# A new order of issue for a bucketed attention and Mish feed-forward kernel on one core

## The chip, the cores and the metric

The kernel runs on one core of a Trainium2 chip. The metric is the device time of one execution in microseconds (us); the median of three runs before the change is 817.67 us (816.54 to 818.07). Engines are named as in the profile: PE (TensorE, matmuls), PEld (its weight loads), DVE (VectorE), ACT (ScalarE), POOL (GpSimd) and SP (SyncE, which here only issues DMAs).

## The reference

Four batches of eight heads, 768 positions, 64 channels. Queries and keys are hashed to six bits each; a query sees only the keys of its own bucket.

```python
q_bits = einsum('bhsd,dk->bhsk', q, proj) > 0          # k_bits in the same way
mask   = q_bucket[:, :, :, None] == k_bucket[:, :, None, :]
scores = where(mask, q @ k.T / sqrt(64), -1e9)
attn   = exp(scores - max(scores)); attn /= sum(attn) + 1e-9
x      = (attn @ v), heads laid side by side           # 3072 x 512
h      = x @ w_in                                      # 512 -> 2048
g      = h * tanh(log1p(exp(h)))                       # Mish
out    = g @ w_out                                     # 2048 -> 512, fp32
```

## The kernel before

The host program does not write instructions straight down. It records 2,636 small operations in a plan (`Plan.op`, L44): each has a name, one or more forms with the engine that each runs on, and the operations that must come before it. Then `Plan.ordered` (L76) walks one long table, `ORDER` (L93): a number is an operation, a letter behind it the form to take (none or a is the first form, b to d the next). The schedule is manual, so each engine's instructions stand in the program in the order in which the table names them, and each engine works through its own row strictly in that order; semaphores between engines come from the recorded dependences. SP issues every DMA, loads and stores and transposes alike, so the transfers queue in table order too. Whenever the next ACT operation needs the other function table (exp or Mish), `ordered` puts a table load (L1315) ahead of it, so the table's order also sets how many loads there are.

The work is cut so that many small pieces interleave. There are 12 units of attention (three for each batch) with eight score blocks each; S0 to S95 count them. One score block goes through this chain:

- S: eight matmuls on PE into a wide PSUM tile `ps_s` (L937; the first blocks in fp32, L948), two heads side by side, 128 queries by 768 keys each. Hash agreement is folded into the product.
- max: one reduction on DVE over 128 x 1536 (L978).
- mb: the scale and the bias for exp, made of the maximum and a threshold. It has four forms: on DVE on both heads at once (L961 and L968), on DVE head by head (two variants, L961 with L968 or L965), or on POOL (L972 and L973).
- exp: two activations on ACT out of `ps_s` (L991), with the row sums.
- rv, hi and lo: the reciprocal (L1021) and the split of the weights into two fp16 parts; hi on POOL (L390), ACT (L392) or DVE (L393), lo on DVE (L408) or POOL (L414, L415).
- transposes by DMA (L472), and for each pair of blocks V: 72 matmuls (L1088).

The feed-forward follows some units behind: X is split (L1096, L1099), H is 24 matmuls (L1130 to L1132), mish runs on ACT (L1147, L1151), its result is split again, and O, an output block, is 6 matmuls for each half (L1179 to L1181), evicted by ACT or DVE (L1197, L1203) and stored (L1207). Between these lie preparations for the next batch: squares for norms on ACT (L480), hash products (L739), splits of inputs and weights.

The start is a chain of its own: loads of K and Q, a unit matrix on POOL (masks.py lines), warm-up matmuls of a tile of ones on PE (L364), transposes on PE against the unit matrix (L450, copied out by L453), a hash projection (L461) by a small matrix `pw` that DVE makes (L530), and the first score blocks in fp32.

Of the kernel before, what the change touches and what calls it, by code (L numbers as in the profile page):

```python
# [93 lines left out]
137 7 9 8 50 20 0 5 11 19 12 22 1 2 3 4 76 80 29 81b 13 37 6 77b 14 15 10 25 33 26 30b 38 17 27 28 18 34 39 52  # L94
60 61 35 62 41 56 54 63 57 55 21 42 48 51 53 24 23 31 78 36 32 64 65 16 86 91 138 92 79 87 147 40 88 82 117 83
43 118 44 119b 93 89 66 109 110 111 153 90 94 120 67 112 154b 132 107d 46 108 133 113 95 115 68 114 116 124
125b 155 121 126 101 84 45 134 136 135 156 127b 178 96 128 140b 148 141 47 58 149 85 122d 123 97 99 142 139b
98b 143 129 168d 179 180d 100 174 176 69 175 177 170 130 157 171b 131 172 173b 204 205b 169 70 145b 182 189
144b 102 158 159 181 161b 190b 71 193 291 194 195 185 191 150 186 192 220 221 103 222d 183b 187 206 160b 196
188 197 104 223 212 152 146 49 151 162 59 105 106 213b 207 216 218 217b 219b 214 215b 184 353 224 243 163 239  # L100
164 244 245b 241 248 240 242 233c 270 368 307 210d 208 235 254 236 255 249 209b 237 246 238 247 225 256 271
250 257 234 272d 262 263 268 266 292 198 273 226 267b 211 227 293 165 294 269 251 283 284 349 350 264 303 265
285 295 166 304b 354 305 296 258 199 200 309d 286b 310 311c 260c 261 306 274 281 313 253 252 232 228 282 312b
322 201 317 364 287 365 288 289 290 366 318 319 355b 323 324 308 320 321 367 330b 331 315 338 339 72 231 203
202 167 229 397 369b 314 329 316 325 297 298b 275 276b 340 333 341 230 332b 334 342 73 370d 299 336 425c 277
# [12 lines left out]
692 628 693d 572 624b 643b 782 672 644 645c 646 695 694 669 610b 658 723c 724 629 630b 684b 687 696 734 735
670b 673 783 697 675 725b 727 736d 738 686 726 631 698 737 688 690 689 732 786 731 749 674 667 699c 701 729
740d 741 791 742c 744 676 728 787 788 700 750 751 702 730 745 799 703 704 706 743b 677b 671 678 746 739 733  # L120
803 781 752 753 773b 800 784c 774 776 775 785 790 679b 804 705b 707 708 710 709 711 794 748 824 712 801c 779
777b 795 796c 802b 789 713 792 714c 716 780 747 778 825 839 680 798 797 816c 817 818b 715b 819 826 827 828 829
820 822 830 807 808 842 611 717 754 755 821 847 823 810 831b 832 833b 809 811 756 757 805 843 844 845 835 846
840 718 859 841 836 834c 719 721b 720b 758 759 860 722 760 837 838 769 861 871 872 863 873b 874 812 862b 864
875 876d 806 813 762 866 793 877 887 891 888 761 889b 892 865 879b 895 763 867 896 897d 898 848 878c 882 890b
880 868 884 904 764 765 885b 893c 899 883 881 849 850c 900 770 923 766b 852b 913b 914 771 767 922 908 924 768
925 905 901 915 916 926 917 927 928c 853 772 909 918 894 919 1026 920 929 930c 906 939 932b 910 902b 911 912
940 814b 869 968 854 921 972 941d 943 942 954 851c 903 931c 934 907 855 857 945 946 856 955 956c 947b 949b 969
973 1027 957 958 959c 937 936 982 970c 1028 933 935 960 961 948b 951b 858 971 963 976 815 944 977 978 979c 950
# [1216 lines left out]
```

## Time and profile before

| | |
|---|---|
| median of the runs | 817.67 us (816.54 to 818.07) |
| profiled execution | 817.2 us, its span 815.4 us, granted clock 1.00 |
| PE busy | 798.2 us (98%) |
| DVE busy | 602.9 us (74%) |
| ACT busy | 624.9 us (77%), of it 150.1 us in 117 table loads |
| POOL busy | 426.9 us (52%) |
| DMA traffic | 134.29 MB, mean 165 GB/s |

All times are from one profiled execution. A row of a timeline gives start, duration, engine, line, operation, result <- operands, shapes, and in brackets the idle time of the engine ahead of it with what ended it. In a list of groups the numbers behind the bar are busy time in us and mean ns of one instruction, then idle time ahead. In a list of waits stand the waiting engine and line, what it waited for, total us, times and the longest. A busy PE is not necessarily PE at its peak, as matmuls overlap: eight score matmuls last 1.46 us alone, but the next block starts 1.30 us after the first.

### The profile page before, as it was taken

To read this page: it belongs to the slowest core of one execution; us is meant where nothing else is said; L and a number is where in the kernel's file an instruction comes from. 1 tells how busy PE (TensorE), PEld (TensorE's weight loads), DVE (VectorE), ACT (ScalarE), POOL (GpSimd) and SP (SyncE) were. 2 spreads that over 40 slices of the span, in tenths; PEclk is the share of its full clock that TensorE was granted. 3 is DMA by queue.
4 is the path that set the end of the run, shared out by engine and by line. 5 is a ranking of instruction groups with operands and counts; after the bars stand their busy time and mean duration, and the time that the engine had idled before them with its cause. 6 is when DMAs were issued, how large, how long until landed. Compare 5 with 4: busy or idle time off the path is not lost.

```text
span 815.4 us, 17000 instructions
## 1 busy us (share of the span) xinstructions
PE 798.2 (98%) x6546; PEld 549.6 (67%) x6546; DVE 602.9 (74%) x1103; ACT 624.9 (77%) x976; POOL 426.9 (52%) x434
## 2 busy tenths in 40 slices
PE   8899999999999999999999999999999999999998
PEld 5556666666676776676666676667676676776674
DVE  5888999988898778887887767768877675566211
ACT  4889998888696769889679698989779785677211
POOL 3564446554356773733585564344646758845120
PEclk9999999999999999999999999999999999999999
DMA  7958998989999969989989959999989577466200
GB/s 253 219 174 221 240 246 196 191 156 206 217 160 182 203 116 181 170 158 216 185 172 155 195 117 151 197 213 192 167 140 169 107 139 145 81 124 133 50 27 27
DMA packets 395489, 134.29 MB, mean 165 GB/s; under 512 B 365456, under 2 KB 386448, under 8 KB 395408
## 3 DMA queue, kind: packets, MB, share of 16 engines
q1 hardware_dynamic: 395408, 133.21, 81.2%
q8 instruction: 51, 0.84, 0.4%
q14 instruction: 30, 0.25, 0.1%
HBM read 35.65 MB, written 6.29 MB: 51 GB/s over the span
## 4 chain that ended last, share of the span: by engine, by line
PE 47%; ACT 1%; DVE 1%; DMA 1%; issue 0%; POOL 0%; SPq 0%; ACTq 0%; DVEq 0%
PE ps_s L937 7%; PE ps_o L1179 6%; PE ps_o L1181 6%; PE ps_o L1180 6%; PE ps_acc L1130 5%; PE ps_t L1088 5%; PE ps_acc L1132 5%; PE ps_acc L1131 5%; ACT pb L991 1%; DVE svb L978 1%; DMA out_dram<-ffb 1%; PE ps_t L739 0%; ACT L1315 0%; DVE hl L408 0%; ACT tok L480 0%
## 5 line engine op out<-in xcount | busy, mean ns | idle before, releaser
L991 ACT ACTIVATE pb<-ps_s,svb 128x768 f32<-128x768 f32 x184 | 180.9, 987 | 87.4 <-DVE svb L968 36.7
L978 DVE TENSOR_REDUCE svb<-ps_s 128x2 f32<-128x1536 f32 x92 | 161.3, 1753 | 40.2 <-PE ps_s L937 33.7
L1130 PE MATMUL ps_acc<-X,wo 128*128 128x256 f16 x616 | 167.9, 273 | 0.3 <-ACT ffb L1151 0.3
L1132 PE MATMUL ps_acc<-X,wo 128*128 128x256 f16 x616 | 167.9, 273 | 0.0
L1131 PE MATMUL ps_acc<-X,wo 128*128 128x256 f16 x616 | 167.9, 273 | 0.0
L1315 ACT ACT_TABLE_LOAD x117 | 150.1, 1283 | 2.0
L408 DVE SCALAR_TENSOR_TENSOR hl<-pb,svb,hl 128x768 f16<-128x768 f32 x131 | 140.3, 1078 | 13.8 <-POOL hl L390 9.8
L1181 PE MATMUL ps_o<-wi,ffb 128*128 128x512 f16 x352 | 133.4, 379 | 0.0
L1180 PE MATMUL ps_o<-wi,ffb 128*128 128x512 f16 x352 | 133.4, 379 | 0.0
L1179 PE MATMUL ps_o<-wi,ffb 128*128 128x512 f16 x352 | 133.4, 379 | 0.0
L937 PE MATMUL ps_s<-KT,QT 128*128 128x512 f16 (+1 forms) x656 | 120.1, 326 | 2.1 <-ACT pb L991 1.8
L390 POOL TENSOR_SCALAR hl<-pb,svb 128x768 f16<-128x768 f32 x68 | 71.0, 1046 | 75.9 <-DVE svb L1021 28.8
L937 PEld LDWEIGHTS <-QT 128*128 128x128 f16 x672 | 64.2, 98 | 40.5 <-issue 8.3
L1088 PE MATMUL ps_t<-PT,VT 128*64 128x256 f16 x1584 | 90.7, 273 | 0.0
L1088 PEld LDWEIGHTS <-VT 128*64 128x64 f16 x1584 | 84.8, 110 | 8.1 <-issue 7.6
L1151 ACT ACTIVATE ffb<-ps_acc,smalls 128x512 f32<-128x512 f32 x88 | 58.5, 684 | 33.5 <-PE ps_acc L1132 32.0
L415 POOL TENSOR_TENSOR hl<-pb,hl 128x768 f16<-128x768 f32 x45 | 75.0, 1667 | 3.8
L414 POOL TENSOR_SCALAR pb<-pb,svb 128x768 f32<-128x768 f32 x45 | 44.4, 987 | 48.0 <-ACT hl L392 21.4
L1131 PEld LDWEIGHTS <-wo 128*128 128x128 f16 x616 | 60.2, 98 | 13.3 <-issue 1.5
L1130 PEld LDWEIGHTS <-wo 128*128 128x128 f16 x616 | 60.2, 98 | 12.6 <-issue 0.5
L1132 PEld LDWEIGHTS <-wo 128*128 128x128 f16 x616 | 60.2, 98 | 7.0
L1181 PEld LDWEIGHTS <-ffb 128*128 128x128 f16 x352 | 34.4, 98 | 41.6
(240 smaller groups left out, 1300.5 us busy)
## 6 DMA issues: line engine op xcount, KB each, us to landing
out_dram<-ffb SPq DMA_DIRECT2D x22, 256.0 KB, 2.7
stg<-in_v_dram SPq DMA_DIRECT2D x13, 384.0 KB, 4.0
stg<-in_k_dram SPq DMA_DIRECT2D x12, 384.0 KB, 4.0
wo<-in_q_dram SPq DMA_DIRECT2D x9, 512.0 KB, 4.9
stg<-in_moe_w_in_dram SPq DMA_DIRECT2D x8, 512.0 KB, 4.6
stg<-in_moe_w_out_dram SPq DMA_DIRECT2D x6, 512.0 KB, 4.6
PT<-hl SPq DMA_TRANSPOSE x176, 4.1
wo<-in_moe_w_out_dram SPq DMA_DIRECT2D x5, 512.0 KB, 4.7
```

The lines of the kernel that those rows point to most:

```text
L408: return [("DVE", 215 + 1.035 * n, port(lambda: nc.vector.scalar_tensor_tensor(out=dst, in0=src, scalar=sc, in1=hi, op0=ALU.mult, op1=ALU. ...
L937: nc.tensor.matmul(ps[:, hh * S + c0 * P:hh * S + c1 * P], QTb[:, u % 2, sl, qi], KTb[:, j, sl, hh * NCH + c0:hh * NCH + c1].rearrange("p ...
L978: op("max", [("DVE", 1755, lambda: nc.vector.tensor_reduce(out=sv[:, 0], in_=ps.rearrange("p (h e) -> p h e", e=S), axis=AX.X, op=ALU.max, ...
L991: EXP[n, hh] = op("exp", [("ACT", 1075, lambda hh=hh, t=t: nc.scalar.activation(pb[:, t], HOMES[n][0][:, hh * S:(hh + 1) * S], AF.Exp, bia ...
L1088: nc.tensor.matmul(pv[hh * D:(hh + 1) * D, y * 256:(y + 1) * 256], vt[:, w, hh * NCH + c], pt[:, hh, a * NCH + c].rearrange("p s t -> p (s ...
L1130: nc.tensor.matmul(o, wh, X[:, 0, c], start=(c == 0), stop=False)
L1131: nc.tensor.matmul(o, wh, X[:, 1, c], start=False, stop=False)
L1132: nc.tensor.matmul(o, wl, X[:, 0, c], start=False, stop=(c == NCC - 1))
L1179: nc.tensor.matmul(PS[f"o{s}"], gh, wh, start=first, stop=False)
L1180: nc.tensor.matmul(PS[f"o{s}"], gh, wl, start=False, stop=False)
L1181: nc.tensor.matmul(PS[f"o{s}"], gl, wh, start=False, stop=last)
L1315: for fn in plan.ordered("exp", lambda x: nc.scalar.preload_act_table_set(sets[x])):
```

## The change

Only the table `ORDER` differs. Both tables name all 2,636 operations once. 2,501 of them stand at another place, by nine places on the mean and 251 at most, and 483 have another letter, that is another form or engine for the same operation. No operation, buffer or transfer is new. Because forms and places differ, so do some counts: the scale and bias (mb) run on POOL 33 times where they ran there 22 times, and ACT has 109 table loads where it had 117.

```diff
 ORDER = """
-137 7 9 8 50 20 0 5 11 19 12 22 1 2 3 4 76 80 29 81b 13 37 6 77b 14 15 10 25 33 26 30b 38 17 27 28 18 34 39 52
...
+8 7 9 50 19 20 12 22 11 18 10 0 1 2 80 3 29 4 33 25 13 37 54 26 34 30b 52 48 60 57 56 17 81b 5 6 31 32 27 38
...
```

First place, DVE at the start. `ones` feeds the warm-ups, `ffb` is the unit matrix here, KT and QT are transposed inputs, pw the hash matrix. Before:

```order
L358 MEMSET ones 128x128
L358 MEMSET floors 128x1
L453 COPY KT<-ps_t 128x384
L358 MEMSET floors 128x4
L453 COPY KT<-ps_l 128x384
L501 TENSOR_SCALAR smalls<-ps_t 128x1
L485 TENSOR_SCALAR smalls<-smalls 128x1
L375 TENSOR_REDUCE smalls<-ffb 128x1
L377 TENSOR_SCALAR smalls<-smalls 128x1
L453 COPY KT<-ps_s 128x384
```

In the change:

```order
L358 MEMSET smalls 128x1
L375 TENSOR_REDUCE smalls<-ffb 128x1
L377 TENSOR_SCALAR smalls<-smalls 128x1
L358 MEMSET ones 128x128
L453 COPY KT<-ps_s 128x384
L530 TENSOR_SCALAR pw<-pj_79 64x6 x4
L453 COPY KT<-ps_t 128x384
```

The reduction over the unit matrix now stands ahead of the memset of ones, and pw behind the first of the three copies; before, pw stood behind all three and four more instructions.

Second place, POOL at the start (`tok_65` is a tile that is cleared once; L972 and L973 are mb). Before:

```order
L795 MEMSET wo 128x12x64
masks.py:197 MEMSET ffb 128x128
masks.py:199 ISA
masks.py:199 AFFINE_SELECT ffb<-ffb 128x128
L358 MEMSET pw 128x128
L358 MEMSET tok_65 128x2048
L390 TENSOR_SCALAR tok_64<-wi,smalls 128x8x64
```

In the change:

```order
L358 MEMSET tok_65 128x2048
masks.py:197 MEMSET ffb 128x128
masks.py:199 ISA
masks.py:199 AFFINE_SELECT ffb<-ffb 128x128
L358 MEMSET pw 128x128
L414 TENSOR_SCALAR PT<-PT,smalls 128x768
L415 TENSOR_TENSOR wo<-PT,wo 128x12x64
L972 TENSOR_SCALAR svb<-svb,smalls 128x2
L973 TENSOR_TENSOR svb<-svb 128x2
L972 TENSOR_SCALAR svb<-svb,smalls 128x2
L973 TENSOR_TENSOR svb<-svb 128x2
L795 MEMSET wo 128x12x64
```

The large clear has moved ahead of the unit matrix, a split of a key tile has come to POOL, and the first two scale-and-bias pairs as well.

Third place, ACT about the score block S24, whose exps are the L991 row behind the last table load of each piece. Before:

```order
L1315 ACT_TABLE_LOAD
L1151 ACTIVATE ffb<-ps_acc_782,smalls 128x512
L392 ACTIVATE hl<-pb,svb 128x768 x2
L392 ACTIVATE VT<-stg,smalls 128x768
L1151 ACTIVATE ffb<-ps_acc_783,smalls 128x512
L480 ACTIVATE tok_64,smalls<-stg 128x768 x2
L1315 ACT_TABLE_LOAD
L991 ACTIVATE pb,svb<-ps_s,svb 128x768 x2
```

In the change:

```order
L480 ACTIVATE tok_64,smalls<-stg 128x768
L1012 ACTIVATE svb<-svb 128x2
L392 ACTIVATE hl<-pb,svb 128x768
L1315 ACT_TABLE_LOAD
L1151 ACTIVATE ffb<-ps_acc_779,smalls 128x512
L480 ACTIVATE tok_64,smalls<-stg 128x768
L1151 ACTIVATE ffb<-ps_acc_780,smalls 128x512
L1315 ACT_TABLE_LOAD
L991 ACTIVATE pb,svb<-ps_s,svb 128x768 x2
```

The two squares (L480) stood together straight ahead of the exp table load; now the first is ahead of the Mish table load and the second between two mish.

More of the change, by code (lines that the diff above doesn't have):

```diff
@@ new lines @@
+350 264 303 265 285 261 304b 199 258 294d 295 296 286b 200 309b 310 311b 355 312b 305 253 167 252 232 203 274
+281b 308 282 306 313 228 322 201 231 323 317 364 287 365 288 289 290 366 318 319 315 324 259 320 321 367 325
+357 338 229 397 399 369b 314 202 330c 297 331 275 339 230 276b 298b 333 332b 334 340 341 342 370d 316 329 328
+335 299 425c 336 277 426 398 300 278 400 302 280 301 337 378 423 424 351 371 373c 379 380 381 372b 374 382
+389c 427 411 376 428 452 390 352 406 407 375 279 391 383 384b 412 451 73 392c 393 74 408d 409 343 410 415d
@@ new lines @@
+628 639 708 572 782 672 643b 641 669 644 645c 646 696 693d 694 695 657b 723d 687 658 624c 667 724 725b 629b
+610 673 734 735 686 727 736d 630b 679b 697 675 737 738 677b 783 726c 689 786 731 690 749 678b 688 728 631 698
+674 699c 701 729 740b 741 670b 742 743 787 750 744 676 751d 733 799 702 730 703 745 700c 790 732 803 739 753
+752 784c 704 706 705b 707 709 671 746b 710 773c 774 776b 775 777 785 791 779 800 801 711 794 748 747 778 780
+712 781 824 795 825 713 796 714c 716 680 788 804 789 797 798 816d 817 819 792 818 826 827 828c 829 820 822 802
@@ new lines @@
+830 807 839 808 810 805 715b 806b 831d 832 809 811 812 754 755 611 717 756 757 821 823 642 847 842 843 844 845
+833b 835 846 860d 840 859 758 841 759 834c 718 836 837 719 861 769 871 872 884 770 891 887 838 863 760b 721b
+720b 862b 722 864 873d 874 875 876d 865 885b 813 771 762 866 772 877 895 888 892 896 763 867 900 764 904 868
+761b 878 848 889 879b 893 897d 882 883 898 880 881 899 849 765 766 894 767 850c 890 913b 914 852 923 924 925
+901 915b 917 916c 902c 926 927 814 922 908 768 853 919 920 918 1026 939 928 929 793 815 905 909 911 910 906b
@@ new lines @@
+1017 870 1223 1195 988b 1070 1018 1038 1196 1082 1073 1042b 1052d 1053 1043 1054 1055c 1044 1056 989 1057c
+1059 1045b 1058c 1046 1060 1077 1061b 1078 1079c 1083 1074 1081 1080 1063 1020 1086 1064 1035b 1067 1068 1071c
+1072 1075c 1197 1036 1084c 1095c 1096 1098b 1097 1099b 1062 1105 1047 1090 1106 1107c 1108 1109 1101 1110 1085
+1111 1121 1122 1087 1091 1048 1076b 1198 1112c 1123 1124 1114 1125 1150 1151 1088b 1127d 1037 1065 1100 1113c
+1158 1116 1102 1154 1136 1104 1103 1128 1092 1200 1155 1137 1115 1117 1129b 1130c 1138 1131 1139 1132 1140
@@ new lines @@
+1141c 1133 1093 1142 1143b 1145 1134 1146 1119 1168 1159 1160 1161 1163 1162 1177c 1144b 1147 1152c 1153 1126
+1118 1164 1178 1094 1169 1179 1187 1188 1189 1190 1181 1191 1207c 1208 1148 1049 1201 1120 1172 1180b 1183b
+1156 1089b 1165 1166 1157b 1209c 1211 1218 1199 1219 1220b 1173 1175 1224 1182 1210b 1213b 1184 1252 1212 1174
+1225 1176 1226c 1222 1221 1236d 1237 1238 1149 1135 1240b 1228 1186 1185 1216 1202 1247 1282 1215 1278 1248
+1249c 1250 1251 1203 1239c 1205 1214 1253 1229 1241 1286 1204b 1242 1267d 1170 1171 1268 1279 1167b 1283 1287
@@ new lines @@
+1269b 1280 1281 1271 1270 1243 1206 1291 1230 1235 1295 1288d 1273 1231 1289 1290 1318 1405 1308b 1227c 1309
+1310c 1233 1312 1254 1255 1284b 1217 1256 1275 1319 1320d 1272 1274 1257 1258 1232b 1260 1311 1321 1322 1338b
+1299 1296 1300 1276b 1304b 1292 1293b 1285 1301 1339 1234 1306 1349 1244 1340b 1259b 1350 1314 1351d 1294b
+1313 1261 1342 1341c 1315 1245 1302 1303 1353 1352 1355c 1401 1397 1356 1305 1344b 1402 1398 1297b 1246 1343
+1324 1345 1323 1364 1365 1366d 1316 1367 1357c 1358c 1359 1368 1325 1326 1418 1262 1317 1409 1361 1388 1263
@@ new lines @@
+1389 1390c 1264b 1265b 1392b 1410 1411b 1406 1399c 1414 1347 1327 1346 1412 1413 1431c 1462 1360 1391c 1394
+1362 1393 1395 1266 1441 1348 1354 1403c 1298 1328 1329c 1432 1331 1442 1443c 1433b 1435 1444 1369 1363 1422
+1332 1307 1400b 1445 1446c 1434c 1437 1370 1415 1423 1447 1425 1419 1416c 1448b 1330b 1450b 1424 1426 1371
+1372 1396 1457 1333 1334 1458 1440 1439 1459b 1373 1502 1374 1335b 1404 1336b 1460 1461 1375 1475 1476 1377
+1438 1436 1449 1451 1486 1337 1378 1506 1477 1503 1504b 1515 1379 1454 1452 1407 1479 1487 1488 1490 1489 1277
@@ new lines @@
+1453 1505 1417 1507 1376b 1478b 1420c 1491 1380 1481 1382b 1381b 1480 1510 1463 1492 1493c 1511 1512d 1464
+1495 1421 1513 1514 1455 1465b 1494c 1497 1528 1529 1408 1384 1467 1383 1482 1496 1519 1456 1498 1468 1641
+1538 1385 1474 1483 1520 1587 1499 1530b 1539 1386 1540 1532 1531c 1508b 1469 1470 1466c 1516 1541 1542 1543c
+1427b 1534b 1471b 1509 1544 1554 1545 1523 1555 1591 1387 1547 1533 1583 1521b 1642 1556d 1558 1524 1557 1569
+1522b 1517 1518b 1546b 1549b 1682 1560c 1472 1526 1500 1537 1484 1588 1525 1561 1570 1571 1548 1563 1584 1536
@@ new lines @@
+1535 1473 1550 1552 1551 1572 1562b 1564 1573 1574c 1597 1559 1428 1527 1566 1429b 1575 1430 1565 1501 1576
+1592 1553 1601 1582 1577 1585c 1578b 1643 1644 1593 1594 1567 1596 1595 1610c 1580 1586 1646 1681 1611 1579
+1568 1620 1618 1621 1645 1598 1613 1599b 1622b 1616 1581 1485 1605 1619 1683 1589 1600 1590 1623 1647 1612b
+1614b 1624 1625 1626 1627c 1629b 1615 1636 1628b 1631b 1633 1634 1635 1606 1637 1607 1638c 1868 1630 1617 1632
+1608 1602 1609 1648 1603 1653 1640 1639 1654c 1655 1656 1657c 1665 1666 1667 1668 1658 1669 1688 1684 1660
@@ new lines @@
+1792c 1783 1747 1767 1759b 1813 1762 1749 1761 1763 1734 1735 1802 1741 1771c 1815 1768 1793 1795 1814 1803
+1804 1805 1787 1764 1794b 1796 1806 1798 1822d 1772b 1823 1824c 1826b 1867 1816 1664 1797 1799 1827 1780 1790
+1839 1788 1833 1801 1750 1834 1835d 1840 1841 1789 1791 1843 1831 1817 1800 1784 1837 1836 1851c 1862 1852
+1853c 1818 1820 1819b 1855b 1854c 1863 1864b 1825 1828 1866 1865 1785b 1781b 1882c 1844 1821 1857 1842c 1782
+1856 1829 1893 1897 1901 1830 1845 1869 1870 1902 1883 1885c 1903 1786b 1884 1858 1680 1832 1904 1886 1905
@@ new lines @@
+2004 1946 2005c 2007 2024 2025 2026c 2028 2027 2046c 1984 1947 1977 2033 1969 1963 2008 1948 2056 1949 2015
+2018 2006b 1945b 1913b 2011 1986 1987 1951 2057 2009b 2010 1950b 2019b 1988 1978 2055 1989 2047 2048c 2034
+2030 2031b 2049 1990c 2058 2050 2060 2059 2061c 1992 2052 1999 2032 2062 2063c 2037 2072 1861 1952 1991b 2038
+2040 2039 2041 1993 2051 2053 2070 1994 2121 2089 2073 2022 2074 2078 2065b 2075 2076 2064b 2122 2090d 2035
+2036b 1995 2067 2079 2080 2091 2092 2066 2101 1892 2068 2102 2103 2093 2104 2094 2105 2106c 2117 2000 2114
@@ new lines @@
+2054 2082 2107 2096 2023 2125 2069 2134 2071 2126 2001 2206 2002 1996b 2127d 2108 2128 2110 2129 2123 2143d
+2095 2097 2083 2118 2109c 2111 2153 2098 2084 2144 2112 2296 2044c 1997 2085 2154 2155c 2145 2146c 2147 2156
+2115b 2042c 2157 2113 2256 1998 2130 2138 2119 2149 2120 2081c 2158b 2159 2160c 2169 2099 2131 2045b 2141
+2132b 2135 2086b 2133b 2162 2170 2171b 2257 2139 2172 2173 2136c 2150 2148 2161c 2043 2087 2175 2124 2164 2176
+2163 2151 2198 2202 2184 2203 2185 2177b 2178 2199 2179 2297 2186 2188 2181 2137 2088 2165 2166 2152 2168 2216
@@ new lines @@
+2316 2288c 2290 2298 2305c 2291 2301b 2311 2325c 2293 2335 2277 2264 2302 2317 2326 2327c 2328c 2329b 2294
+2336 2337b 2338 2339 2292 2320 2330 2351 2334 2384 2340c 2313 2306 2341 2318 2319b 2331b 2342 2349 2352 2353
+2354 2323 2344 2355 2357c 2343c 2321 2366 2332 2266b 2314 2265 2278b 2333 2315 2346 2385 2358 2367 2368b 2369
+2345 2359b 2361 2370 2371d 2360b 2372 2347 2373c 2375 2267 2363 2356 2348 2362 2376 2364 2380 2386b 2381 2382b
+2350 2389 2398 2394 2379 2365 2374 2377b 2383b 2322 2390 2391 2392 2393 2407c 2324 2408 2409c 2417 2418 2419
@@ new lines @@
+2411 2420 2421 2378 2402 2403 2422c 2423 2387b 2416 2405 2412 2433 2395 2410c 2404 2406 2424 2426b 2413 2434
+2414 2435c 2436 2437 2439b 2425 2396c 2397 2415 2431 2466 2430 2450 2467 2440 2428 2427 2451 2442b 2468b 2441
+2399 2443 2400 2452c 2445 2453 2454 2429 2279 2438 2401 2479 2470 2480 2471 2444 2295 2455 2456 2457c 2472
+2432 2481b 2458 2461b 2459 2474 2447 2463 2475 2476c 2478 2477 2446 2448 2483 2460 2462 2502 2547 2469 2492d
+2464b 2493 2495 2473b 2503 2504d 2505 2494 2498b 2496 2506 2507c 2508 2487 2500 2518 2449 2497 2501 2484 2548
@@ new lines @@
+2519 2520c 2510c 2499 2551 2515 2509b 2511b 2482 2485c 2513 2514 2512 2522 2521 2524c 2549c 2525 2486 2550b
+2533 2516 2555 2523 2517 2546 2488 2552 2527b 2530b 2490 2526 2528 2553c 2534 2535 2537 2536 2538b 2539 2529
+2541b 2544 2540 2554b 2532 2569 2568 2556 2557b 2558b 2542 2531 2465 2489 2491 2559 2570 2560 2571 2545 2543
+2561c 2562 2572 2573 2563 2577 2574 2564 2565 2566 2567 2580 2581 2582 2584 2585 2586c 2583b 2588 2592 2589
+2578b 2575b 2590c 2593 2594b 2587b 2591b 2595b 2597 2596 2599 2608 2601 2598 2603 2600 2604 2602 2609 2605
@@ L210 @@
+2606b 2610c 2607 2612 2611b 2613 2621 2616 2614 2615 2623 2620 2625 2622 2576 2579 2617 2618 2619 2631 2634b
+2635 2632b 2633 2624 2626 2629b 2627b 2630 2628
 """
```

153 lines of the change are left out of this document (38 added, 115 removed).

## The prediction

> **What bounds the kernel now.** I read the page's shares first, then the windows, then what TensorE waits for.
>
> ```profile
> PE 798.2 (98%) x6546; PEld 549.6 (67%) x6546; DVE 602.9 (74%) x1103; ACT 624.9 (77%) x976; POOL 426.9 (52%) x434
> ...
> PE 47%; ACT 1%; DVE 1%; DMA 1%; issue 0%; POOL 0%; SPq 0%; ACTq 0%; DVEq 0%
> ```
>
> TensorE is busy for 98% of a span of 815.4 us, and the chain that ended last runs over it almost alone. No order takes a matmul away, so only TensorE's idle time can move. It is spread as follows (columns: window, its length, then busy time of PE, PEld, DVE, ACT and POOL, granted clock, DMA share, GB/s).
>
> ```profile
> 0.00:75.00 75.00, 66.44 (x556) 44.26 (x557) 56.83 (x124) 57.09 (x113) 38.17 (x49) 1.00 0.79 217
> 75.00:310.00 235.00, 231.40 (x1810) 161.22 (x1809) 205.46 (x351) 195.40 (x301) 126.05 (x124) 1.00 0.95 192
> 310.00:767.00 457.00, 455.76 (x3883) 314.85 (x3880) 332.70 (x616) 363.95 (x550) 255.09 (x253) 1.00 0.84 157
> 767.00:815.40 48.40, 44.60 (x306) 29.27 (x300) 7.94 (x14) 8.50 (x14) 7.56 (x9) 0.99 0.06 22
> ```
>
> Length less PE busy gives 8.56, 3.60, 1.24 and 3.80 us of idle: 17.2 us in all. The profiled execution took 817.2 us (the median of the runs shown is 817.67), so an order without any gap would end at 817.2 - 17.2 = 800.0. Half of the prize lies before 75 us; the last window's idle is mostly the last eviction and store, after the last matmul. These are the waits with a name, first of the start, then of 75 us to the end (total, times, longest):
>
> ```profile
> PE ps_l L461 <- DVE pw L530: 1.2, 1, 1.2
> ...
> PE ps_s L937 <- ACT pb L991: 1.8, 5, 0.6
> PE ps_t L739 <- DVE hl L408: 0.7, 1, 0.7
> ```
>
> After 75 us the largest is a score block S that waits until the block before it has been through exp (L991), which frees its PSUM.
>
> **The change part by part.** The 2,636 operations are the same; numbers and letters of the order alone differ. So TensorE's own work costs the same, and each term below is a wait removed or added.
>
> *1. The start.* Before:
>
> ```profile
> 0.71 0.74 POOL L795 MEMSET wo<- 128x768 f16 x1 [0.29 <-POOLq L1330]
> ...
> 2.05 1.80 POOL L358 MEMSET tok<- 128x2048 f16 x1
> 0.81 0.17 DVE L358 MEMSET ones<- 128x128 bf16 x1 [0.81 <-PEq L1330]
> 1.03 3.60 PE L364 MATMUL ps_l<-ones 128*128 128x128 bf16 x32 [1.03 <-DVE floors L358]
> 4.56 1.48 PE L450 MATMUL ps_l<-ffb,wi 128*64 128x128 f32 x12
> 9.07 1.59 DVE L530 TENSOR_SCALAR pw<-pj 64x6 f32<-64x6 f32 x4
> 10.81 1.09 PE L461 MATMUL ps_l<-QT,pw 128*128 128x512 f32 x2 [1.23 <-DVE pw L530]
> 14.89 1.58 PE L948 MATMUL ps_s<-KT,QT 64*128 64x256 f32 x8
> ```
>
> The hash projection at 10.81 waited 1.23 us for pw, the last of a row of DVE instructions. The new order puts pw sixth on DVE, ahead of the second transposed copy: that wait can go (gain 0 to 1.23; I take 0.8, since the transposes that feed the same matmul still come first). Against it, POOL now clears tok first, where it began with L795, and DVE's maximum over the unit matrix stands ahead of the memset of ones. Between L795's end (1.45) and tok's start (2.05) lie 0.6 us, in which POOL made the matrix; behind tok it is ready at about 0.71 + 1.80 + 0.6 = 3.1, and the first warm-up, behind three short DVE instructions, at about 3.5 instead of 1.03. That is 2.5 us, and the warm-ups now stand among the first transposes (L450), which began at 4.56. Each of the 32 takes 3.60/32 = 0.11 us, so 2.5 us of them can slide in front of the transposes, or fill gaps in which these wait for loads. I take 0.5 lost (0 to 2.5). The scores' first scale and bias (mb) now go to POOL: of S0 to S8 all but S5 do. Each costs up to the price of term 3 while TensorE has little else to do; I take 0.6 (0 to 3). Net: +0.3 us.
>
> *2. S24 to S27.* Before:
>
> ```profile
> 206.11 1.46 PE L937 MATMUL ps_s<-KT,QT 128*128 128x512 f16 x8 [0.57 <-ACT pb L991]
> 207.50 4.12 PE L1088 MATMUL ps_t<-PT,VT 128*64 128x256 f16 x72
> 212.03 1.46 PE L937 MATMUL ps_s<-KT,QT 128*128 128x512 f16 x8 [0.41 <-ACT pb L991]
> ...
> 201.76 0.84 ACT L480 ACTIVATE tok<-stg 128x768 bf16<-128x768 f32 x1 [0.62 <-DMA stg<-in_v_dram]
> ...
> 202.71 1.28 ACT L1315 ACT_TABLE_LOAD   x1
> 204.01 0.99 ACT L991 ACTIVATE pb<-ps_s,svb 128x768 f32<-128x768 f32 x1
> 204.99 0.98 ACT L991 ACTIVATE pb<-ps_s,svb 128x768 f32<-128x768 f32 x1
> ```
>
> ACT stood on a square whose input landed late, then loaded the exp table, then did both exps of S24; S25 waited 0.57 us for them. The new order parts the two squares, has SP issue the inputs of both earlier (the first by a whole score block), and leaves one square and a mish straight ahead of the load. TensorE has four output blocks between S24 and S25, 4 x 1.30 = 5.2 us; the chain from an S's end over maximum and scale to the second exp's end takes 4.6 (term 3's rows: 601.54 - 596.93), so the wait should go if the table is loaded in time. S26 stood behind V10 alone and waited 0.41; it now has V10 and one more output block (1.30) ahead. The two are 0.98 of the 1.8 us in this group. I take -1.0 (-1.8 to 0).
>
> *3. Scale and bias on POOL.* This is the one group of edits that puts a longer link into a chain that TensorE waits for: 22 of these pairs ran on POOL, and 33 do now; eleven (S56 and S64 among them) go back to DVE and 22 come over. The prices of DVE's form, then of POOL's (minimum, median, maximum ns for POOL):
>
> ```profile
> L961 DVE TENSOR_SCALAR svb<-svb,smalls 128x2 f32<-128x2 f32 x37 | 11.1, 300 | 0.9
> L968 DVE TENSOR_TENSOR svb<-svb 128x2 f32<-128x2 f32 x37 | 7.0, 190 | 1.3
> ...
> L972 POOL TENSOR_SCALAR svb<-svb,smalls x22: 295/922/1390, 34.1 to 689.1; 128x2 f32<-128x2 f32 x22
> ...
> L973 POOL TENSOR_TENSOR svb<-svb x22: 193/466/859, 34.5 to 690.3; 128x2 f32<-128x2 f32 x22
> ```
>
> DVE takes 0.49 us, POOL 0.49 at best, 1.39 at the medians, 2.25 at worst. What makes POOL slow shows at S56, where both of its instructions run beside a DVE pair of L408:
>
> ```profile
> 446.44 1.95 DVE L408 SCALAR_TENSOR_TENSOR hl<-pb,svb,hl 128x768 f16<-128x768 f32 x2
> ...
> 446.64 0.99 POOL L972 TENSOR_SCALAR svb<-svb,smalls 128x2 f32<-128x2 f32 x1 [1.54 <-DVE svb L978]
> 447.71 0.73 POOL L973 TENSOR_TENSOR svb<-svb 128x2 f32<-128x2 f32 x1
> ```
>
> [...]
>
> Whether that matters is set by what TensorE does meanwhile. Take S76, which moves from DVE to POOL:
>
> ```profile
> 595.63 1.46 PE L937 MATMUL ps_s<-KT,QT 128*128 128x512 f16 x8
> ...
> 598.22 0.27 PE L1130 MATMUL ps_acc<-X,wo 128*128 128x256 f16 x1
> ...
> 600.84 0.38 PE L1179 MATMUL ps_o<-wi,ffb 128*128 128x512 f16 x1
> ...
> 602.14 1.46 PE L937 MATMUL ps_s<-KT,QT 128*128 128x512 f16 x8
> ...
> 597.20 1.76 DVE L978 TENSOR_REDUCE svb<-ps_s 128x2 f32<-128x1536 f32 x1 [0.44 <-ACT ffb L1151]
> 599.00 0.33 DVE L961 TENSOR_SCALAR svb<-svb,smalls 128x1 f32<-128x1 f32 x2
> ...
> 599.58 0.99 ACT L991 ACTIVATE pb<-ps_s,svb 128x768 f32<-128x768 f32 x1 [1.12 <-DVE svb L965]
> 600.56 0.98 ACT L991 ACTIVATE pb<-ps_s,svb 128x768 f32<-128x768 f32 x1
> ```
>
> The second S starts at 602.14; ahead of it stand an output block of 1.30 us (from 600.84), an H of 2.62 (from 598.22) and another output block, so that S76 itself ends at 596.93. From S76's start to the second exp's end is 601.54 - 595.63 = 5.91 us, of which the step from the maximum's end (598.96) to the first exp is 0.62. The next S starts 6.51 after the first, without a wait: 0.6 to spare. With POOL at its median that step grows by 1.39 - 0.49 = 0.9, which is 0.3 too late; at worst by 1.76, 1.2 too late; at best by nothing. TensorE's work between two neighbouring S is mostly longer: counted over both orders by these blocks (and 4.1 for a V) it is 6.4 us on the mean in either. Behind a pair on POOL it is short at six places: S52, S62 and S76 (5.2), S33, S47 and S8 (5.4 to 5.5). Three at 0.4 and three at 0.2 make 1.8. S66 ran before with a POOL pair and 5.5 us of cover, and none of L937's five waits is behind it, so I take half: +0.9 (0 to 6 x 1.2 = 7.2).
>
> *4. The rest.* The new order has 109 table loads where there were 117:
>
> ```profile
> L1315 ACT ACT_TABLE_LOAD x117 | 150.1, 1283 | 2.0
> ```
>
> That is 8 x 1.28 = 10.3 us less on ACT, and by the same means some 14 us less on POOL and 8 more on DVE. I cost this at nothing, because TensorE's 455.76 busy of 457 us in the long middle hides it; if ACT were late there, the gain would be at most that window's 1.24 us. S55 and S61 get the DVE form or keep it with similar cover; other short waits (the hash transposes at L739, 0.7) move with their neighbours: -0.8 (-3 to +1). After 767 us TensorE's blocks stay dense and the same two evictions come last: nothing.
>
> Sum: +0.3 - 1.0 + 0.9 - 0.8 = -0.6 us; 817.2 - 0.6 = **816.6 us**. The median of the runs is 0.47 above the profiled execution, within their own spread (816.54 to 818.07), and I add nothing for it.
>
> **The rivals.** A is the sum: small gains and small losses that nearly cancel.
>
> B, slower: POOL's scale and bias decides. A pair that comes behind a longer instruction on POOL is late by that too. If the six short places pay 0.7 to 1.2 each, 4.2 to 7.2 us, and the start pays 1 of its 3, against gains of 1.5 to 2: between +3 and +6, some 821 us. It decides as soon as the pairs take their median and the maximum is not early; S66 without a wait speaks against it, the POOL rows' median of 922 against 295 for it.
>
> C, faster: both gains are full (start 1.2, S24 to S30 1.8, other named waits 2) and POOL's pairs are hidden, as nearly all were before: 817.2 - 5 = 812.2. For it: 8.56 us of idle in the start, where order decides most. Against it: what stands there is a chain of loads, transposes and copies, each waiting for the one before.
>
> D: the order changes nothing that the chip's engines would not have done anyway, since each engine only keeps its own order and TensorE's is nearly the same: 817.2 to 817.7.
>
> [...]
>
> **How the numbers follow.** A 0.50, B 0.25, C 0.19, D 0.06. A measurement of this kernel tells 0.2%, 1.6 us, from no change. A's own range is 814 to 819; 44% of it lies below 816.0, 44% within 1.6 of 817.67, and 12% above. So faster: 0.19 + 0.5 x 0.44 = 0.41; slower: 0.25 + 0.5 x 0.12 - 0.02 for the part of B that falls short = 0.29; the same: 0.30, with D in it. The range takes in most of B and C: 811 to 821.5.
>
> **What would show it.** In the profile after: no wait of L461 for pw, or one under 0.6; no wait of L937 for L991 between 195 and 215 us; L972 some 33 times with a median near 0.9 us, and waits of L937 at S52, S62 and S76 of 0.2 to 0.7 each. PE busy stays at 798 and idle at 16 to 17 us. I am wrong if the idle before 75 us moves by over 2 us, if ACT's shorter work shortens the middle by more than its 1.24, or if L937's total wait for L991 rises over 4 us.

## The result: slower, by one wait above all

The changed kernel takes 825.13 us (median; 822.06 to 827.06), before 817.17 us over the same number of runs (816.54 to 818.07). The ratio is 1.0094, with a 95% interval of 1.0075 to 1.0114. The forecast was 816.6 us, a little faster, with a range of 811 to 821.5; the kernel became slower. Ratios here and below leave out slow executions, of which there was one, 1182.63 us for the last variant, where its other ten lie between 816.47 and 819.85.

The shares of the changed kernel's page:

```profile
PE 799.9 (97%) x6546; PEld 550.1 (67%) x6546; DVE 608.1 (74%) x1080; ACT 612.2 (74%) x966; POOL 401.2 (49%) x429
```

ACT and POOL did get lighter, by 12.7 and 25.7 us, and DVE heavier by 5.2. None of that shows in the time. TensorE's busy time rose by 1.7 us although it does the same matmuls, and its idle time from 17.2 to 823.3 - 799.9 = 23.4 us. The windows of the changed kernel, with the same columns and limits as before:

```profile
0.00:75.00 75.00, 66.15 (x553) 43.60 (x554) 54.55 (x119) 56.85 (x115) 35.33 (x52) 1.00 0.79 220
75.00:310.00 235.00, 230.25 (x1806) 160.84 (x1806) 200.58 (x341) 196.74 (x301) 125.46 (x127) 1.00 0.94 192
310.00:767.00 457.00, 450.95 (x3801) 310.95 (x3799) 343.98 (x607) 350.75 (x540) 228.95 (x239) 1.00 0.84 156
767.00:823.30 56.30, 52.55 (x392) 34.75 (x389) 8.97 (x16) 7.89 (x12) 11.49 (x14) 1.00 0.09 27
```

Idle is now 8.85, 4.75, 6.05 and 3.75 us. Start and end are nearly as they were (8.56 and 3.80 before); the second window, which had 3.60, has 4.75, and the long middle, which had 1.24, has 6.05. The largest named waits of TensorE in the whole run, the second of them at the start:

```profile
PE ps_s L937 <- ACT pb L991: 7.4, 9, 2.5
PE ps_l L364 <- DVE ones L358: 3.6, 1, 3.6
PE ps_t L496 <- ACT tok L480: 1.4, 2, 0.9
```

The first was 1.8 us over five times; now it is 7.4 over nine, beyond the 4 us that the prediction had named as a sign of its being wrong, and a single wait has 2.5 of it. That one stands between S58 and S59. TensorE before:

```profile
459.04 1.47 PE L937 MATMUL ps_s<-KT,QT 128*128 128x512 f16 x8
465.53 1.46 PE L937 MATMUL ps_s<-KT,QT 128*128 128x512 f16 x8
472.47 1.46 PE L937 MATMUL ps_s<-KT,QT 128*128 128x512 f16 x8
```

TensorE after (S58, S59, two of the H matmuls behind it, S60):

```profile
459.20 1.46 PE L937 MATMUL ps_s<-KT,QT 128*128 128x512 f16 x8
...
468.78 1.78 PE L937 MATMUL ps_s<-KT,QT 128*128 128x512 f16 x8 [2.54 <-ACT pb L991]
470.35 0.42 PE L1130 MATMUL ps_acc<-X,wo 128*128 128x256 f16 x1
...
473.38 0.27 PE L1130 MATMUL ps_acc<-X,wo 128*128 128x256 f16 x1
...
476.99 1.46 PE L937 MATMUL ps_s<-KT,QT 128*128 128x512 f16 x8
```

S58 starts 0.16 us later than before: up to here, 56% of the span, the new order had neither won nor lost. S60 starts 476.99 - 472.47 = 4.52 later. The wait is only part of the 4.4 us lost between S58 and S60; matmuls behind it ran slow. The clock that TensorE was granted in 466 to 475 us (the number behind POOL's busy time), first of the changed kernel, then of before:

```profile
466.00:475.00 9.00, 6.46 (x40) 4.49 (x38) 5.12 (x8) 5.91 (x11) 0.14 (x1) 0.81 0.31 58
```

```profile
466.00:475.00 9.00, 9.00 (x85) 7.01 (x84) 5.05 (x11) 6.49 (x13) 6.85 (x6) 1.00 0.69 131
```

A narrower window of the changed kernel finds the slow stretch; ahead of it (466 to 469.78) and behind it (473.19 to 480) the clock is 1.00:

```profile
469.78:473.19 3.41, 3.41 (x17) 2.19 (x15) 2.61 (x5) 0.61 (x2) 0.00 (x0) 0.50 0.00 0
```

So 3.41 us of work went at half the clock. That costs about 1.7 us, as much as TensorE's busy time rose.

What did ACT do meanwhile? After:

```profile
458.03 0.47 ACT L1096 ACTIVATE X<-ps_t,smalls 128x256 f16<-128x256 f32 x1 [0.25 <-PE ps_t L1088]
462.88 0.47 ACT L1096 ACTIVATE X<-ps_t,smalls 128x256 f16<-128x256 f32 x1 [4.38 <-DVE X L1099]
463.38 1.28 ACT L1315 ACT_TABLE_LOAD   x1
464.67 0.69 ACT L1151 ACTIVATE ffb<-ps_acc,smalls 128x512 f32<-128x512 f32 x1
465.38 1.28 ACT L1315 ACT_TABLE_LOAD   x1
466.67 0.99 ACT L991 ACTIVATE pb<-ps_s,svb 128x768 f32<-128x768 f32 x1
467.65 0.98 ACT L991 ACTIVATE pb<-ps_s,svb 128x768 f32<-128x768 f32 x1
```

And DVE after:

```profile
460.70 1.76 DVE L978 TENSOR_REDUCE svb<-ps_s 128x2 f32<-128x1536 f32 x1 [1.86 <-PE ps_s L937]
462.37 0.48 DVE L1099 SCALAR_TENSOR_TENSOR X<-ps_t,smalls,X 128x256 f16<-128x256 f32 x1
```

ACT wanted to evict the second half of X and waited 4.38 us for DVE's x_lo of the first half. DVE was free, but the new order had put x_lo behind the maximum of S58, whose scores came only at 460.7. Behind the waiting eviction stood a table load, a mish, another table load and only then the exps that free `ps_s` for S59. ACT before, for the same stretch:

```profile
459.18 0.47 ACT L1096 ACTIVATE X<-ps_t,smalls 128x256 f16<-128x256 f32 x1
462.99 0.99 ACT L991 ACTIVATE pb<-ps_s,svb 128x768 f32<-128x768 f32 x1 [3.34 <-DVE svb L968]
463.98 0.98 ACT L991 ACTIVATE pb<-ps_s,svb 128x768 f32<-128x768 f32 x1
464.94 0.47 ACT L1096 ACTIVATE X<-ps_t,smalls 128x256 f16<-128x256 f32 x1
```

There the exps came first, with the exp table in place, and the second eviction after them. That a second eviction waits for the x_lo ahead of it shows in the kernel before as well, at one other place and for 0.31 us only (x_lo ran there from 242.17 to 242.65):

```profile
242.69 0.47 ACT L1096 ACTIVATE X<-ps_t,smalls 128x256 f16<-128x256 f32 x1 [0.31 <-DVE X L1099]
```

### The profile page after: what moved, and what is told of

Read it like the earlier page. It is cut to its first block, busy times and chain, and to the rows that moved or that the text cites. A ratio compares the mean times of both kernels' runs of the same rounds, so it can differ in the third digit from the quotient of the medians.

```text
span 823.3 us, 16985 instructions
## 1 busy us (share of the span) xinstructions
PE 799.9 (97%) x6546; PEld 550.1 (67%) x6546; DVE 608.1 (74%) x1080; ACT 612.2 (74%) x966; POOL 401.2 (49%) x429
## 5 line engine op out<-in xcount | busy, mean ns | idle before, releaser
L991 ACT ACTIVATE pb<-ps_s,svb 128x768 f32<-128x768 f32 x184 | 180.9, 986 | 100.2 <-DVE svb L968 54.4
L408 DVE SCALAR_TENSOR_TENSOR hl<-pb,svb,hl 128x768 f16<-128x768 f32 x135 | 141.6, 1057 | 15.0 <-ACT hl L392 6.0
L390 POOL TENSOR_SCALAR hl<-pb,svb 128x768 f16<-128x768 f32 x58 | 64.0, 1103 | 95.8 <-DVE svb L1021 59.1
L415 POOL TENSOR_TENSOR hl<-pb,hl 128x768 f16<-128x768 f32 x41 | 68.9, 1680 | 3.4
L414 POOL TENSOR_SCALAR pb<-pb,svb 128x768 f32<-128x768 f32 x41 | 40.2, 981 | 52.6 <-ACT hl L392 33.0
L392 ACT ACTIVATE hl<-pb,svb 128x768 f16<-128x768 f32 x56 | 51.7, 930 | 16.2 <-DVE svb L1021 4.9
```

The source lines that it names most:

```text
L408: return [("DVE", 215 + 1.035 * n, port(lambda: nc.vector.scalar_tensor_tensor(out=dst, in0=src, scalar=sc, in1=hi, op0=ALU.mult, op1=ALU. ...
L991: EXP[n, hh] = op("exp", [("ACT", 1075, lambda hh=hh, t=t: nc.scalar.activation(pb[:, t], HOMES[n][0][:, hh * S:(hh + 1) * S], AF.Exp, bia ...
```

## The experiments

**One number back.** Two operations swap places in the new order: x_lo (1607) and the maximum of S58 (1637).

```diff
-... 1635 1606 1637 1607 1638c 1868 ...
+... 1635 1606 1607 1637 1638c 1868 ...
```

> One number moved in the new order: the x_lo of the first half (L1099) goes back ahead of the maximum of S58 on DVE. Theory 1 (over half of the loss is one wait: at S59 TensorE stood 2.54 us because ACT's second X eviction, L1096, waited 4.38 us for this x_lo, with two table loads, a mish and both exps of S58 queued behind it; the matmuls after that gap then ran slow for another 1.4 us or so): 4.4 us come back, 825.1 becomes about 820.7; L937's wait for L991 falls from 7.4 to under 5.0 us. Rival (the gap only moves to the next place, because ACT or DVE is late there anyway): under 1 us comes back.

Measured: 820.61 us (ratio to before 1.0041, 1.0025 to 1.0057); 4.5 us came back (4.3 by the two ratios). ACT and TensorE in it:

```profile
458.95 0.47 ACT L1096 ACTIVATE X<-ps_t,smalls 128x256 f16<-128x256 f32 x1 [0.74 <-DVE X L1099]
...
462.90 0.99 ACT L991 ACTIVATE pb<-ps_s,svb 128x768 f32<-128x768 f32 x1 [0.17 <-DVE svb L965]
...
465.79 1.46 PE L937 MATMUL ps_s<-KT,QT 128*128 128x512 f16 x8
```

The eviction goes 3.9 us sooner, the table loads and the mish fit under the maximum, and S59 starts without a wait. Theory 1 stands for 4.5 of the 8.0 us.

**The same by the other partner.** Instead of x_lo, the second eviction (1608) moves, ahead of x_lo.

```diff
-... 1606 1637 1607 1638c ... 1632 1608 1602 ...
+... 1606 1637 1608 1607 1638c ... 1632 1602 ...
```

> The new order with one number moved: ACT's second X eviction (L1096) goes ahead of the first x_lo instead of behind it. The two write different columns of X, and the plan knows no dependence between them; by the trace the eviction waits only because it stands behind x_lo in the program. Theory 1 in full (that wait alone holds the table loads, the mish and the exps): the 4.38 us wait on ACT goes, the gap ahead of S59 with it, and the time is about that of the first run, 820.6. Rival (ACT's queue was late for its own length, two table loads between V26 and the exps of S58): 823 or more.

Measured: 820.61 us again (1.0026 to 1.0057). The plan's own dependences do not ask for that wait, or this order could not have been given. The wait exists only when the eviction stands behind x_lo in the program. The two share the tiles X and `ps_t`, in different columns; which of the two brings the wait no run here shows.

**The wait put into the kernel before.**

```diff
-... 1612 1602 1613b ... 1616 1603c 1624 ... 1606 1607 1637 1638b 1604 ... 1640 1639 1608 ...
+... 1612 1613b ... 1616 1624 ... 1606 1637 1607 1638b 1608 1602 1603c 1604 ... 1640 1639 ...
```

> The kernel before with the wait of S58 put in: x_lo behind the maximum of S58, the second X eviction behind it, and one mish of the block before between that and the exps (five numbers moved, same table loads). Theory 1: S59 waits about 3 us for the exps, and the matmuls after it run slow for 1.4 to 1.7 us: 817.2 becomes 821.5 to 822. Rival (idle time alone, no slow matmuls): about 820.2. Rival (slack at the next blocks takes it back): under 818.5.

Measured: 821.13 us, ratio 1.0047 (1.0032 to 1.0062), 4.4 us over its own before. S59, and the window of 466 to 475 us:

```profile
468.18 2.72 PE L937 MATMUL ps_s<-KT,QT 128*128 128x512 f16 x8 [2.92 <-ACT pb L991]
```

```profile
466.00:475.00 9.00, 6.82 (x60) 5.06 (x60) 4.41 (x10) 5.33 (x11) 5.26 (x5) 0.81 0.42 80
```

The same mechanism costs the same in the other kernel. S59 itself took 2.72 instead of 1.46 us, about half speed. Here the stretch at clock 0.50 runs from 467.62 to 471.03, so its first 0.56 us still fall into the gap.

**A shorter wait.** As above, but with the mish (1602) ahead of the second eviction (1608) and a square (1809) behind it.

```diff
-... 1606 1607 1637 1638b 1604 ...
+... 1606 1637 1607 1638b 1602 1608 1809 1603c 1604 ...
```

> As the fourth run, but the mish goes ahead of the second X eviction and a square comes in behind it, so that by the before trace's durations TensorE stands about 1.85 us ahead of S59 instead of 2.9. If every gap costs slow matmuls in proportion: +2.9 us (1.85 and about 1 more), 819.6 to 820. If only a gap beyond some length between 1.1 and 2.5 us slows them: +1.9 and none slow, 818.6.

Measured: 818.82 us, ratio 1.0013 (1.0002 to 1.0025). S59 and the same window:

```profile
467.40 1.46 PE L937 MATMUL ps_s<-KT,QT 128*128 128x512 f16 x8 [1.76 <-ACT pb L991]
```

```profile
466.00:475.00 9.00, 7.60 (x77) 6.28 (x77) 3.80 (x11) 5.76 (x11) 6.11 (x6) 1.00 0.46 87
```

TensorE stood 1.76 us, and nothing behind it ran slow: S59 is 1.87 us late, about the gap. From S58 to S60 the changed kernel and the run above take 4.36 us longer than without their gaps of 2.54 and 2.92 us (17.79 instead of 13.43 us): the gap's own length and 1.8 or 1.4 us on top. Half of the slow work is 3.41/2 = 1.7 and (3.41 - 0.56)/2 = 1.4.

**Five scale-and-bias pairs by letter alone.** The letters of S13, S33, S47, S52 and S62 change from d (POOL) to none (DVE).

```diff
-432d 1007d 1366d 1512d 1738d
+432 1007 1366 1512 1738
```

> Five letters changed in the new order: the scale and bias of S13, S33, S47, S52 and S62 from POOL back to DVE. Theory 2 (the pairs on POOL cost what stands ahead of S14, S34, S48, S53 and S63 in the trace: 1.2, 1.0, 0.2, 0.5 and 0.9 us, 3.8 in all, less what later slack gave back): 3 to 4 us come back, about 821.6. Rival (the chain behind these pairs is late for other reasons, the maximum or the exps' own queue): under 1 us comes back.

Measured: 830.42 us, ratio 1.0159 (1.0137 to 1.0181): 5 us slower than the changed kernel, the opposite of both theories. The pairs kept their places in the order, and those were chosen for POOL. S13's now queues on DVE behind eight instructions, from 100.60 to 105.02 us. S14, and the clock in 105 to 112 us:

```profile
108.38 2.72 PE L937 MATMUL ps_s<-KT,QT 128*128 128x512 f16 x8 [2.62 <-ACT pb L991]
```

```profile
105.00:112.00 7.00, 4.38 (x24) 2.49 (x21) 3.55 (x9) 5.73 (x10) 3.62 (x3) 0.76 1.08 237
```

The gaps ahead of S34 and S63 grew too, from 0.92 to 2.46 and from 0.74 to 1.88 us. The one ahead of S34 is as long as others here that slowed TensorE, but the clock stayed at 1.00 behind it:

```profile
276.87 1.46 PE L937 MATMUL ps_s<-KT,QT 128*128 128x512 f16 x8 [2.46 <-ACT pb L991]
```

```profile
276.87:280.00 3.13, 3.13 (x17) 1.66 (x17) 1.71 (x6) 2.58 (x6) 2.18 (x2) 1.00 0.25 48
```

**The same five, directly behind their maxima.** Those of S47 and S52 stood there already; the other three move, as at S13 (maximum 431, pair 432).

```diff
-... 431 327 377 417c ... 396 401 432d 434 ...
+... 431 432 327 377 417c ... 396 401 434 ...
```

> The second run's edit without its confusion: the scale and bias of S13, S33, S47, S52 and S62 go from POOL to DVE and, in the order of numbers, directly behind their maxima (before, only the letter was changed, so they queued on DVE behind what stood between, up to five instructions). Theory 2 (POOL's pairs cost about 1 us each where cover is short): the waits ahead of S14, S34, S53 and S63 shrink by 1.0, 0.9, 0.5 and 0.5 us; 825.1 becomes about 822. Rival (DVE is as late as POOL at these places): 824.5 or more.

Measured: 822.66 us, ratio 1.0061 (1.0037 to 1.0086). That is 2.5 us less than the changed kernel, though the two intervals overlap, and 0.85 us of the difference in the two traces already lies ahead of S12, where nothing was changed. What the trace shows of the five: the way from S13 to S14 got shorter by 0.9 and that from S52 to S53 by 0.5 us; the gaps ahead of S34 and S63 did not shrink, S34's grew by 0.6. So theory 2 holds for two places of five, for some 1.4 us, or 0.9 with S34's loss against it.

**The letters alone in the old sequence.**

```diff
-ORDER: old numbers, old letters
+ORDER: old numbers, new letters (483 differ)
```

> The old sequence of numbers with the new letters: which engine and form an operation takes changes, nothing moves. If the forms carry the loss (rival B, POOL's pairs), this is slower than before by 3 us or more, 820 to 824. If the sequence carries it (theory 1), it stays within 2 us of before's 817.2; I expect +1 to +3, since some pairs on POOL will meet little cover here too.

Measured: 958.07 us, ratio 1.173 (1.171 to 1.175). TensorE's largest wait:

```profile
PE ps_s L937 <- ACT pb L991: 60.3, 39, 4.7
```

Neither sequence nor forms can be said to carry the change: a form is good only at the place it was chosen for. The run decides nothing between rival B and theory 1.

**All named gaps mended.** Beside x_lo and the five pairs: a hi (1926) behind S69's maximum and scale, S73's scale behind its maximum, a g_hi (1699) behind S62's scale, a load (709) ahead of a transpose (707) on SP, ones (0) and the unit matrix first at the start.

```diff
-... 706 705b 707 709 671 ... 1898 1926c 1927b 1934 1860 1935b 1906 ... 2057 2009b ... 1990c 2058 2050 ...
+... 706 705b 709 707 671 ... 1898 1927b 1934 1860 1935b 1926c 1906 ... 2057 2058 2009b ... 1990c 2050 ...
```

> The new order with every named gap mended by moving numbers: x_lo ahead of the maximum of S58 (4.4 us measured), the five scale-and-bias pairs on DVE behind their maxima (2.9), one hi of S69's row behind its maximum instead of ahead of it (0.8), S73's scale and bias directly behind its maximum (0.5), one g_hi behind S62's scale (0.3), one input load ahead of a transpose on SP (0.9), and ones and the unit matrix first at the start (0.5). If the losses are these separate places, they add up: 825.1 - 10.3 = about 815, below before's 816.7. If slack elsewhere was hiding others, less: 817 to 820.

Measured: 818.42 us, ratio 1.0011 (1.0000 to 1.0021): 6.7 of the hoped-for 10.3 us. Two gaps are gone as reckoned: S70's, 0.74 us in the changed kernel and 0.73 or 0.74 in the five other variants of the new order traced without this mend, and S74's, 0.60 us; but S74's was between 0 and 0.47 in those five, so its mend is not shown to be the cause. What had delayed S70 shows in the changed kernel, DVE first, then POOL:

```profile
545.64 1.91 DVE L393 TENSOR_SCALAR hl<-pb,svb 128x768 f16<-128x768 f32 x1 [1.99 <-DMA PT<-hl]
547.47 1.75 DVE L978 TENSOR_REDUCE svb<-ps_s 128x2 f32<-128x1536 f32 x1
```

```profile
545.50 1.64 POOL L415 TENSOR_TENSOR hl<-pb,hl 128x768 f16<-128x768 f32 x1
```

A hi that mostly takes 0.62 us on DVE had waited 1.99 us for a transfer and then took 1.91, 0.41 beyond the end of POOL's L415 (547.14), and S69's maximum stood behind it. POOL's L415 had started 0.14 us ahead of it. In the traces of the kernel before and of the changed one, the seven hi (L393, 128x768) that ran beside an L415 for 0.49 us or more took 0.91 to 1.91 us and ended 0.40 to 0.42 us behind it; one of the changed kernel that started 0.15 us ahead of an L415 (at 487.62) took 0.61. In this mended kernel S34's gap was 1.51 us (0.92 in the changed kernel), though its scale was early. ACT, DVE and POOL:

```profile
267.54 0.99 ACT L991 ACTIVATE pb<-ps_s,svb 128x768 f32<-128x768 f32 x1 [0.61 <-DVE svb L968]
270.28 0.99 ACT L991 ACTIVATE pb<-ps_s,svb 128x768 f32<-128x768 f32 x1 [1.66 <-DVE hl L408]
```

```profile
267.68 1.51 DVE L393 TENSOR_SCALAR hl<-pb,svb 128x768 f16<-128x768 f32 x1
269.23 1.02 DVE L408 SCALAR_TENSOR_TENSOR hl<-pb,svb,hl 128x768 f16<-128x768 f32 x1
```

```profile
267.50 1.28 POOL L415 TENSOR_TENSOR ffb<-ffb 128x512 f16<-128x512 f32 x1
```

The first exp went early, the second had to wait for the hi and lo of an earlier block to free its output buffer. The same hi in the changed kernel:

```profile
268.19 0.62 DVE L393 TENSOR_SCALAR hl<-pb,svb 128x768 f16<-128x768 f32 x1
```

There its lo ended at 269.86 and POOL's pair at 269.90, so neither would have held the exps much longer than the other. Without the pair POOL's L415 came earlier, started 0.18 us ahead of the hi, and the hi took 1.51 instead of 0.62 us, ending 0.41 us behind it here too. Taking the pair from POOL lost here what it should have won.

Before S24 the mends did win: S24's first matmul came at 196.12 instead of 197.63 us. But its other seven then waited 1.34 us for transposed queries, a wait that the changed kernel did not have.

**The start alone.**

```diff
-8 7 9 50 ... 18 10 0 1 2 ...
+0 7 9 8 50 ... 18 10 1 2 ...
```

> The new order with two numbers moved at the start: the memset of ones comes first on DVE and the clear of tok behind the unit matrix on POOL, so the warm-ups start at about 1 us instead of 3.6. Term 1 of the prediction charged the late warm-ups 0.5 us: S12 then starts 0.3 to 0.7 us sooner (88.53 in the new order, 87.84 before). Rival (loads and copies set the start, not warm-ups): S12 moves by under 0.2 us.

Measured: 824.31 us, ratio 1.0075 (1.0050 to 1.0101), not to be told from 825.13. S12 starts at 87.34 instead of 88.53 us, but in four other kernels with the new start untouched it came at 88.12, 88.43, 87.68 and 88.73, so a single trace settles this to about half a microsecond at best. Two more variants have the same mend of the start, the mended kernel above and the one below, and their S12 came at 87.97 and 86.88. The mean of the three is 87.4, that of the five with the new start as it was (88.53 among them) 88.3: some 0.9 us, still few traces, for the late warm-ups.

**Mended again.** On top of the mended kernel: one hash copy (1030) behind S33's hi and lo, a square (1810) behind S62's exps, the load (709) yet one transpose earlier, a V transpose (838) behind the keys' transpose (722).

```diff
-... 703 745 700c ... 709 707 ... 1006 1007 1030c 997c 999 ...
+... 703 709 745 700c ... 707 ... 1006 1007 997c 999 1030c ...
```

> The sixth run's kernel after a look at the gaps left in it: at S33 one hash copy goes behind the hi and lo that free the exp buffers (ACT's second exp waited 1.75 us for them although the scale was early), at S62 a square goes behind the exps, ahead of which it stood with the table load, the late input load goes one transpose further up, and one transpose for V goes behind the transposed keys that S28 waited for. If each gap is one misplaced instruction, 0.3 + 1.2 + 0.8 + 0.8 us come back: 818.4 becomes about 815.3, below before's 817. If every mend only uncovers the next wait, it stays at 817.5 or more.

Measured: 817.86 us, ratio 1.0010 (0.9999 to 1.0022): no gain that can be told. S63's gap went, and S34's fell to 1.0 us. But S24 now came so early that it waited longer still for its transposed queries:

```profile
195.11 0.38 PE L937 MATMUL ps_s<-KT,QT 128*128 128x512 f16 x1
197.58 1.50 PE L937 MATMUL ps_s<-KT,QT 128*128 128x512 f16 x7 [2.09 <-DMA QT<-tok]
```

```profile
197.00:203.00 6.00, 5.42 (x22) 2.36 (x23) 4.38 (x8) 2.66 (x5) 2.00 (x2) 0.72 1.04 198
```

After 2.09 us of standing the clock fell there too, to 0.50 from 198.46 to 201.87. What the earlier places had won was lost at the next chain. No version tried here beats the kernel before.

## Why the prediction was wrong

**The bound** was read rightly: TensorE bounds the kernel, apart from the 1.7 us of half clock only its idle time moved, and no gain from ACT's lighter load or the eight table loads saved shows in the time.

**Term 1, the start (+0.3).** Right in size as far as the traces tell: S12 starts 0.69 us late in the one pair of traces, but the three kernels with the old start have it at 87.84, 88.25 and 88.26, 88.1 on the mean, and the five with the new start at 88.3. The wait for pw is gone, as said, and a 3.6 us wait for ones has come ahead of the warm-ups. The start mended alone and in two other variants speaks for a price of the late warm-ups of 0.9 rather than 0.5.

**Term 2, S24 to S27 (-1.0).** The 0.57 and 0.41 us waits ahead of S25 and S26 are gone, as reckoned, and a wait for a square's input ahead of the hash sums (L496, 0.9) has come instead. By S58 all gains and losses together stood at +0.16 us; the sum of the first three terms had been +0.2. That is chance as much as skill, since term 3 had its places wrong.

**Term 3, the pairs on POOL (+0.9).** The place list was poor. S76, the worked example, shows no wait, nor does S8; S13 behind a V block was not on the list, and of the gaps behind pairs on POOL its was the longest, 1.13 us. The price itself was off as well: in the new order most pairs run near their best.

```profile
L972 POOL TENSOR_SCALAR svb<-svb,smalls x33: 295/344/1256, 19.6 to 737.7; 128x2 f32<-128x2 f32 x33
```

The median fell from 922 to 344 ns. What I had read from S56 alone shows at more places: in each of the two traces eight L972 ran beside an L408 on DVE for over 0.8 us, and these took 0.98 to 1.39 us. Before, they and three beside an L607 (1.19 to 1.33) were half of the 22; after, they are eight of 33, and the other 25 took 0.29 to 0.86. Of the gaps that I would have blamed on POOL, some 1.4 us are shown to be its doing (S14 and S53).

**Term 4, the rest (-0.8, from -3 to +1): this step failed.** I let "the other waits move with their neighbours" and costed ACT's table loads by their total alone. In it lay the 4.5 us of S58, and S70, S74 and other places, each under 1 us. The big one could have been worked out from the rows of before, the 0.31 us wait at 242.69 among them. Behind S58 the new order has on DVE the maximum (1.75) and x_lo (0.48), then on ACT the second eviction (0.47), a table load (1.28), a mish (0.69), a load (1.28) and two exps (1.97): 7.9 us and some 0.3 of hand-overs. TensorE's work between S58 and S59 is four output blocks and a hash product, 4 x 1.30 + 0.45 = 5.65. The difference is 2.5 us, and 2.54 were measured. I had checked this chain with the links of the kernel before, maximum, scale, exp, at S24 and S76, and not with the links that the new order puts into it at each S.

**The rivals.** B gave the right side and about half of the loss (821), by the wrong mechanism: that it came closest is luck, since the pairs on POOL are some 1.4 of 8.0 us, or 0.9 net. 4.5 of them are the wait at S59 with its slow matmuls, shown three ways (taken out by either partner, put into the kernel before); S70's 0.7 is shown by its mend. The rest, between 1 and 2 us, is argued only from the gaps in the trace (S63 and S74, transposed keys at S28 and S78, a square at the hash sums).

## What to carry to other kernels

A change of order has to be checked on every in-order engine at every place where the bounding engine waits: write down what now stands ahead of the releasing instruction, table loads included, and add it up against the cover. An instruction that waits blocks everything behind it, as ACT's second eviction did here for 4.38 us, with two table loads, a mish and two exps behind it, so a move of one place past a waiting instruction can cost 4.5 us, where eight table loads fewer brought nothing that shows. And a form (which engine) must be moved together with its place: with letters and places mixed, the kernel lost up to 17%.

## What the hardware showed that was not expected

TensorE's granted clock can fall after a gap that is short beside the span, but the length of the gap alone does not decide it. In the traces of the changed kernel and of the variants, gaps of 2.09, 2.54, 2.62 and 2.92 us were followed by a clock of 0.72 to 0.81 in windows of 6 to 9 us, with score blocks of up to 2.72 instead of 1.46 us; a gap of 1.76 us was not. Yet the gap of 2.46 us ahead of S34, shown above, left the clock at 1.00, and in the run with the letters alone a gap of 3.16 us (181.75 to 184.91) did so too, while one of 1.93 us (62.09 to 64.02) was followed by 6.83 us at 0.50. Between 1.9 and 3.2 us both happen in these traces.

Nor does the slow stretch begin at a fixed point: it began 1.0 us after the gap's end in the changed kernel, 0.88 after it at S24 in the last run, and 0.56 ahead of it in the kernel before with the wait put in. In these three it lasted 3.41 us at a clock of 0.50. What else than the length of a gap decides whether the clock falls is not shown: no run here varies the place of a gap alone.
